# A third PSUM bank for every third accumulation of a product, borrowed from the attention

## The chip, the cores and the metric

The kernel runs on one core of a Trainium2 chip. The metric is the device time of one execution in microseconds (us). Time is told as the median of several runs; the profile is of one further execution.

## The reference

Three stages follow one another: an attention with a sliding window of 128 keys and four "sink" keys that every query sees, a dense layer with a maximum over three products (a maxout), and a mixture of eight experts in which tokens are assigned greedily by score, 384 to each expert.

```python
# q, k, v: 4 x 8 x 768 x 64
scores = scale * q @ k.T;  keep = is_sink | in_window
a = softmax(where(keep, scores, -1e9));  attn = a @ v
x = attn.transpose(0, 2, 1, 3).reshape(3072, 512)
h = maximum(maximum(x @ w1, x @ w2), x @ w3)      # 3072 x 768
x = h @ w_out                                     # 3072 x 512
logits = x @ w_gate                               # 3072 x 8
# greedy: by falling logit, a token takes the expert if it has room (384)
out[mask_e] = maximum(x[mask_e] @ u1[e], 0) @ u2[e]
```

All of it is in fp32. The kernel reaches that precision by splitting an operand into a high and a low part and adding three products (high by high, high by low, low by high).

## The kernel before, in words

The 3072 tokens are worked off in eight groups of 384 (`g` = 0 to 7). Each group needs four attention units ("pairs", two heads for half of a sequence). For a pair, `score` makes the scores (L138 to L141), which are copied with the mask into a tile T (L144 to L150); `soft` makes the softmax (L156 to L163); `pv` transposes the weights and multiplies them with the values (L166 to L201). In `pv` the weights of the sinks are transposed first, into the tile `pt` (L166, L167; the transposes run at L25): one PSUM bank, of which the pool `pst` has only one. ScalarE reads it at L169, then VectorE at L170, and with that the bank is free again.

The dense layer of a group has two parts. `group` makes the hidden rows: six slices of 128 columns, for each of them three products of 12 matmuls (L305) in the two banks of the tile `mm`, with the maximum taken on ScalarE and VectorE (L307, L308) and the split into high and low parts (L313, L314). `x2` multiplies the hidden rows with w_out: three blocks of 128 tokens, each in two halves of columns, so six accumulations of 18 matmuls (L330). Each accumulates in one bank of `mm` and is copied to the tile `xo` by ScalarE (L332), after which its bank may be written anew. In the middle groups (1, 0, 2, 3, 4 in this order of time) a half has 260 columns: 256 of the output and 4 of the logits, since w_out is kept with the product of w_out and w_gate beside it. Group 0's hidden rows were spilled to DRAM and come back one by one (L347 to L350) when group 1 is done. The last groups go other ways (L362, and L330 with 256 columns) and are not touched.

The eight PSUM banks are divided so in this part: `mm` 2, `pt` 1, `pp` 1 (transposed window weights), `ps` 3 (scores), `po` 1 (product with the values).

The order on each engine is not written out. It is made when the program is built: a scheduler lays instructions out over a simulated timeline, by their priority and as soon as their inputs and a free buffer are there. The four pairs of group g+1 are issued between the slices of group g (L698) with a higher priority, `off` = 60 (L681). On the chip every engine then works off its own queue in the order found, with semaphores for the waits.

Of the kernel before, what the change touches and what calls it, by code (L numbers as in the profile page):

```python
# [19 lines left out]
FT=mybir.dt.float32; FR=mybir.dt.float32r; BF=mybir.dt.bfloat16; I32=mybir.dt.int32; U8=mybir.dt.uint8; U32=mybir.dt.uint32  # L20
AF=mybir.ActivationFunctionType; OP=mybir.AluOpType; AX=mybir.AxisListType
NEG=-8.0e9
def f32(ap): return ap.bitcast(FT)
# [11 lines left out]
class Attn:  # L35
    def __init__(s, tc, q,k,v,vs, keep, consts, pst, psp, pss, psv, work):
        s.tc=tc; s.nc=nc=tc.nc; s.q,s.k,s.v,s.vs=q,k,v,vs
        s.pst,s.psp,s.pss,s.psv,s.w=pst,psp,pss,psv,work
        jp=work.tile([128,128],I32,name="jp",tag="qs0",bufs=2)
        nc.gpsimd.iota(jp,pattern=[[1,128]],base=0,channel_multiplier=-1)  # L40
        s.ident=keep.tile([128,128],FR,name="ident")
        nc.vector.tensor_scalar(s.ident,jp,0.0,None,op0=OP.is_equal)
        s.ca=consts.tile([128,2,128],U8,name="ca")
        nc.vector.tensor_scalar(s.ca[:,0,:],jp,0.0,None,op0=OP.is_le)
        nc.vector.tensor_scalar(s.ca[:,1,:],jp,0.0,None,op0=OP.is_gt)
        s.ul=consts.tile([128,2,128],BF,name="ul")
        nc.vector.tensor_scalar(s.ul[:,0,:],jp,0.0,None,op0=OP.is_lt)
        nc.vector.tensor_scalar(s.ul[:,1,:],jp,0.0,None,op0=OP.is_ge)
        s.negs=consts.tile([128,2,4],FT,name="negs"); nc.vector.memset(s.negs,NEG)

        s.vk=[]; s.pb=[]
        for i in range(2):
            t=consts.tile([128,2,128],FR,name=f"vk{i}"); nc.vector.memset(f32(t),0.0); s.vk.append(t)
            t=consts.tile([128,384],FR,name=f"psb{i}"); nc.vector.memset(f32(t),0.0); s.pb.append(t)
        s.kf=[]; s.ql=[[consts.tile([128,384],FR,name=f"ql{h}") for h in range(2)]]
        t=consts.tile([1,1],FT,name="one"); nc.vector.memset(t,0.0)
        nc.scalar.activation(t,t,AF.Exp)
        s.behind=None; s.ev={}; s.n=0; s.no=('kh0','kh1')
        s.extra=None
# [159 lines left out]

class Moe1:  # L220
    def __init__(s, tc, words,wgate, consts, wpool, main, conv, mm, pt, pss, ident):
        s.tc=tc; s.nc=tc.nc; s.mm=mm; s.pss=pss; s.main=main; s.conv=conv; s.ident=ident; s.consts=consts
        s.src=words; s.wgate=wgate
        s.W=[[wpool.tile([128,4,768],FR,name=f"w{i}{x}") for x in "hl"] for i in range(3)]
        s.WO=None; s.at=None; s.stage=None; s.HL=None; s.nx=0; s.second=None; s.n=0; s.loads=[]
        s.WG=main.tile([128,6,16],FR,name="wgt")
# [92 lines left out]
    def x2(s,H,t0,LG,x2d,n=260,pool=None,keep=None):  # L319

        nc=s.nc; main=s.main; mms=[]
        for t in range(3):
            o=pool.tile([128,512],FT,name="xq",bufs=4) if pool else s.room(t).tile([128,520],FT,name="xo",bufs=1)
            for u in range(2):
                c=slice(0,260) if n==260 else slice(4-4*u,260-4*u)
                ps=s.mm.tile([128,512],FT,name="mm")
                k=0
                for f in range(6):
                    for a,b in ((0,0),(0,1),(1,0)):
                        mms.append(nc.tensor.matmul(ps[:,:n],H[f][a][:,t*128:(t+1)*128],s.WO[b][:,f,u,c],start=(k==0),stop=(k==17))); k+=1  # L330
                with s.tc.high_priority():
                    nc.scalar.activation(o[:,u*n:(u+1)*n],ps[:,0:n],AF.Copy)  # L332
                    if keep is not None:
                        for d in (2*u,2*u+1):
                            h,l=keep(t,d); c=ps[:,(d-2*u)*128:(d-2*u)*128+128]
                            nc.scalar.activation(h,c,AF.Copy)
                            nc.vector.tensor_tensor(l,c,f32(h),op=OP.subtract)
            if n==260:
                o,e=s.row(o,0)
                nc.scalar.activation(LG[:,t0+t,:].rearrange("p (u e) -> p u e",u=2),e,AF.Copy)  # L340
            nc.scalar.dma_start(x2d[(t0+t)*128:(t0+t+1)*128,:],o)
        return mms
# [474 lines left out]
```

## Time and profile before

| what | value |
| --- | --- |
| median of 3 runs | 962.07 us (961.85 to 962.66) |
| the profiled execution | 963.42 us |
| its span, first to last instruction | 961.6 us |
| TensorE busy (PE) | 927.3 us, 96% of the span |
| VectorE busy (DVE) | 705.2 us, 73% |
| ScalarE busy (ACT) | 487.7 us, 51% |
| GpSimd busy (POOL) | 257.1 us, 27% |
| mean granted TensorE clock | 0.992 |

Times in the rows count from the start of the span. A row of a timeline has the start, the duration, the engine, the line of the kernel, the operation, the tile written and the tile read, and the count; in brackets stands how long the engine was idle just before and what ended that. Names such as `T_w` and `T_x` are two buffers of the same tile, and `HL` holds the hidden rows. The five calls of `x2` with 260 columns lie at 173.8 to 193.5 us (group 1), 195.8 to 224.1 (group 0), 279.6 to 296.4 (group 2), 347.8 to 366.3 (group 3) and 417.8 to 434.8 (group 4).

### The profile page before, as it was taken

To read this page: it belongs to the slowest core of one execution; us is meant where nothing else is said; L and a number is where in the kernel's file an instruction comes from. 1 tells how busy PE (TensorE), PEld (TensorE's weight loads), DVE (VectorE), ACT (ScalarE), POOL (GpSimd) and SP (SyncE) were. 2 spreads that over 40 slices of the span, in tenths; PEclk is the share of its full clock that TensorE was granted. 3 is DMA by queue.
4 is the path that set the end of the run, shared out by engine and by line. 5 is a ranking of instruction groups with operands and counts; after the bars stand their busy time and mean duration, and the time that the engine had idled before them with its cause. 6 is when DMAs were issued, how large, how long until landed. Compare 5 with 4: busy or idle time off the path is not lost.

```text
span 961.6 us, 18493 instructions
## 1 busy us (share of the span) xinstructions
PE 927.3 (96%) x6552; PEld 850.4 (88%) x6552; DVE 705.2 (73%) x1867; ACT 487.7 (51%) x1329; POOL 257.1 (27%) x271
## 2 busy tenths in 40 slices
PE   5999899989999999999999999999999999999996
PEld 4688799979999999999999998888888888888895
DVE  7776787687887886778896445888989889874320
ACT  5366474687677675676674211334434434344431
POOL 4676536132321312211231000011103022054321
PEclk9999899999999999999999999999999999999999
DMA  7454321242123121122210002544345353454410
GB/s 233 137 191 144 105 93 64 81 145 68 52 63 94 41 85 57 44 79 85 81 57 1 1 1 88 192 145 132 111 154 176 103 169 119 151 194 156 142 66 33
DMA packets 54443, 99.35 MB, mean 103 GB/s; under 512 B 7792, under 2 KB 24688, under 8 KB 54352
## 3 DMA queue, kind: packets, MB, share of 16 engines
q1 hardware_dynamic: 44464, 75.90, 25.3%
q0 software_dynamic: 3840, 12.45, 3.7%
q10 hardware_dynamic: 6048, 9.83, 2.7%
q8 instruction: 51, 0.84, 0.4%
q14 instruction: 40, 0.33, 0.1%
HBM read 82.17 MB, written 16.12 MB: 102 GB/s over the span
## 4 chain that ended last, share of the span: by engine, by line
PE 82%; DVE 6%; issue 5%; ACT 3%; DMA 2%; POOL 1%; SPq 0%; POOLq 0%; ACTq 0%; DVEq 0%
PE mm L305 28%; PE mm L634 13%; PE acc L627 12%; PE mm L330 8%; PE po L198 3%; PE rc L432 3%; PE po L188 2%; PE pt L25 2%; PE ps L138 2%; PE pp L25 2%; PE ps L140 1%; PE ps L141 1%; PE acc L362 1%; PE po L199 1%; DMA qf<-in_q_dram 1%
## 5 line engine op out<-in xcount | busy, mean ns | idle before, releaser
L627 PE MATMUL acc<-wbh,HL 128*128 128x512 f32 x384 | 133.1, 401 | 0.1
L308 DVE TENSOR_TENSOR hm<-mm,hm 128x384 f32<-128x384 f32 x96 | 53.2, 554 | 50.7 <-PE mm L305 49.5
L330 PE MATMUL mm<-woh,HL 128*128 128x260 f32 (+1 forms) x432 | 86.0, 289 | 2.7 <-ACT xo L332 1.2
L627 PEld LDWEIGHTS acc<-wbh,HL 128*128 128x128 f32 x384 | 71.4, 188 | 12.6 <-ACT HL L637 0.4
L578 ACT ACTIVATE wah<-sa 128x512 fp32r<-128x512 f32 x64 | 40.5, 632 | 82.2 <-PE mm L634 69.3
L578 ACT ACTIVATE wbh<-sb 128x512 fp32r<-128x512 f32 x64 | 40.4, 631 | 72.8 <-PE acc L627 68.9
L627 PE MATMUL acc<-wbl,HL 128*128 128x512 f32 x192 | 76.5, 398 | 0.0
L646 POOL DMA_INDIRECT out_dram<-og,idx x24 | 29.3, 1221 | 168.7 <-ACT og L645 165.9
L330 PEld LDWEIGHTS mm<-woh,HL 128*128 128x128 f32 x432 | 68.4, 188 | 4.7 <-ACT xo L332 1.9
L634 PE MATMUL mm<-HL,wah 128*128 128x384 f32 x256 | 67.5, 341 | 0.0
L305 PE MATMUL mm<-xh,w2h 128*128 128x384 f32 x192 | 66.8, 348 | 0.2 <-ACT hm L307 0.2
L305 PE MATMUL mm<-xh,w1h 128*128 128x384 f32 x192 | 66.1, 344 | 0.8 <-ACT hm L307 0.5
L305 PE MATMUL mm<-xh,w0h 128*128 128x384 f32 x192 | 66.5, 346 | 0.0
L305 PE MATMUL mm<-xl,w0h 128*128 128x384 f32 x192 | 65.4, 341 | 0.0
L305 PE MATMUL mm<-xl,w2h 128*128 128x384 f32 x192 | 65.4, 340 | 0.0
L305 PE MATMUL mm<-xh,w2l 128*128 128x384 f32 x192 | 65.3, 340 | 0.0
L305 PE MATMUL mm<-xh,w1l 128*128 128x384 f32 x192 | 65.3, 340 | 0.0
L579 DVE TENSOR_TENSOR wbl<-sb,wbh 128x512 fp32r<-128x512 f32 x64 | 45.2, 706 | 27.1 <-ACT wbh L578 27.0
L305 PE MATMUL mm<-xh,w0l 128*128 128x384 f32 x192 | 64.9, 338 | 0.0
L305 PE MATMUL mm<-xl,w1h 128*128 128x384 f32 x192 | 64.8, 338 | 0.0
L638 DVE SCALAR_TENSOR_TENSOR HL<-mm,HL 128x384 fp32r<-128x384 f32 x64 | 35.5, 554 | 38.1 <-ACT HL L637 37.8
L163 POOL TENSOR_TENSOR T_w<-T_w,l 128x792 f32<-128x792 f32 x21 | 32.7, 1559 | 108.0 <-DVE l L162 108.0
(334 smaller groups left out, 2815.8 us busy)
## 6 DMA issues: line engine op xcount, KB each, us to landing
sa<-in_u_dram SPq DMA_DIRECT2D x64, 256.0 KB
sb<-in_u_dram SPq DMA_DIRECT2D x64, 256.0 KB
HL<-in_words_dram SPq DMA_DIRECT2D x18, 512.0 KB
qn<-in_q_dram SPq DMA_DIRECT2D x88, 96.0 KB
x2d<-xo ACTq DMA_DIRECT2D x15, 256.0 KB
kn<-in_k_dram SPq DMA_DIRECT2D x12, 264.0 KB
st<-in_words_dram SPq DMA_DIRECT2D x6, 512.0 KB
vn<-in_v_dram SPq DMA_DIRECT2D x12, 256.0 KB
```

The lines of the kernel that those rows point to most:

```text
L25: nc.tensor.transpose(out,x,f32(ident))
L163: s.ev['s',u['n']]=nc.gpsimd.tensor_tensor(T,T,l[:,:,None].to_broadcast([128,6,132]),op=OP.mult)
L198: nc.tensor.matmul(po[:,q:q+n],u['VS'][:,blk,128*h:128*h+128],part[:,c:c+n],start=(part is H and j==0),stop=False,skip_group_check=True)
L305: nc.tensor.matmul(ps[:,:384],s.W[i][a][:,p,f*128:(f+1)*128],X[p][b],start=(n==0),stop=(n==11)); n+=1
L308: else: nc.vector.tensor_tensor(m,ps[:,:384],m,op=OP.max)
L330: mms.append(nc.tensor.matmul(ps[:,:n],H[f][a][:,t*128:(t+1)*128],s.WO[b][:,f,u,c],start=(k==0),stop=(k==17))); k+=1
L578: nc.scalar.activation(h,src,AF.Copy)
L579: (nc.gpsimd if s.n>=6 and nm=="wa" else nc.vector).tensor_tensor(l,src,f32(h),op=OP.subtract)
L627: s.mms.append(nc.tensor.matmul(acc[t],H[f][a][:,t*128:(t+1)*128],W[f][1][b],start=(f==0 and n==0),stop=(f==F-1 and n==2))); n+=1
L634: s.mms.append(nc.tensor.matmul(ps[:,:384],W[f][0][a][:,k,:],X[k][b],start=(n==0),stop=(n==11))); n+=1
L638: nc.vector.scalar_tensor_tensor(l,ps[:,:384],0.0,f32(h),op0=OP.max,op1=OP.subtract)
L646: st=nc.gpsimd.indirect_dma_start(out=s.out,out_offset=bass.IndirectOffsetOnAxis(ap=idx[:,t:t+1],axis=0),in_=o,in_offset=None)
```

## The change

In `x2`, with 260 columns, the third and the sixth accumulation of a group take the tile `pt` from the pool `pst` in place of a tile `mm`. The pool of that name is given to `Moe1` already and only has to be kept. The operations, their shapes, their operands and their number stay the same.

```diff
 class Moe1:
     def __init__(s, tc, words,wgate, consts, wpool, main, conv, mm, pt, pss, ident):
-        s.tc=tc; s.nc=tc.nc; s.mm=mm; s.pss=pss; s.main=main; s.conv=conv; s.ident=ident; s.consts=consts
+        s.tc=tc; s.nc=tc.nc; s.mm=mm; s.pss=pss; s.pt=pt; s.main=main; s.conv=conv; s.ident=ident; s.consts=consts
...
             for u in range(2):
                 c=slice(0,260) if n==260 else slice(4-4*u,260-4*u)
-                ps=s.mm.tile([128,512],FT,name="mm")
+                ps=s.pt.tile([128,512],FT,name="pt") if n==260 and (2*t+u)%3==2 else s.mm.tile([128,512],FT,name="mm")
                 k=0
```

## Rows read from the trace of the kernel before

**Rows 1.** The page's first part: busy time of the engines, share, instructions.

```profile
PE 927.3 (96%) x6552; PEld 850.4 (88%) x6552; DVE 705.2 (73%) x1867; ACT 487.7 (51%) x1329; POOL 257.1 (27%) x271
```

**Rows 2.** Table of stretches; columns named in its first line.

```profile
core 0: us, PE busy (x) PEld busy (x) DVE busy (x) ACT busy (x) POOL busy (x), PEclk, DMA share, GB/s
...
200.00:224.50 24.50, 21.37 (x157) 18.90 (x156) 21.23 (x41) 19.98 (x73) 7.53 (x6) 1.00 0.40 124
224.50:279.60 55.10, 55.10 (x366) 54.79 (x366) 45.99 (x95) 38.93 (x118) 15.51 (x20) 1.00 0.21 60
347.80:366.50 18.70, 17.67 (x148) 17.39 (x146) 16.44 (x31) 14.06 (x46) 5.15 (x6) 1.00 0.31 97
417.70:434.60 16.90, 16.30 (x133) 15.83 (x133) 11.04 (x27) 12.85 (x46) 4.67 (x5) 1.00 0.26 84
434.60:512.00 77.40, 75.51 (x489) 73.48 (x488) 65.90 (x116) 53.05 (x163) 20.09 (x20) 1.00 0.22 67
```

**Rows 3.** TensorE's waits, 173 to 512 us: total, times, longest.

```profile
PE po L198 <- DVE x L201: 1.4, 2, 0.8
PE mm L330 <- ACT xo L332: 1.2, 2, 1.0
...
PE pp L25 <- DVE A_w L179: 0.5, 1, 0.5
```

**Rows 4.** Chain that ended last, near 220 us: start, duration, what (two accumulations).

```profile
219.66 4.39 PE mm L330 x36
```

**Rows 5.** Timelines of VectorE, ScalarE and TensorE in group 0's product.

```profile
203.59 0.55 DVE L170 TENSOR_TENSOR psb<-pt,psb 8x384 fp32r<-8x384 f32 x1
...
209.15 0.56 DVE L350 TENSOR_TENSOR HL<-hm,HL 128x384 fp32r<-128x384 f32 x1
...
213.66 0.55 DVE L29 TENSOR_TENSOR xl<-x,xh 128x384 fp32r<-128x384 f32 x1
...
211.25 0.66 ACT L332 ACTIVATE xo<-mm 128x260 f32<-128x260 f32 x2
...
210.79 0.39 PE L140 MATMUL ps<-kh_w,qs 128*128 128x260 f32 x1 [0.52 <-DVE T_w L150]
...
212.72 0.39 PE L140 MATMUL ps<-kh_w,qs 128*128 128x260 f32 x1 [1.43 <-DVE T_x L150]
```

**Rows 6.** Timelines of VectorE and TensorE ahead of and in group 4's product.

```profile
408.32 0.55 DVE L170 TENSOR_TENSOR psb<-pt,psb 8x384 fp32r<-8x384 f32 x1
...
423.05 0.50 PE L330 MATMUL mm<-woh,HL 128*128 128x260 f32 x2 [0.41 <-DVE HL L314]
...
424.14 0.39 PE L330 MATMUL mm<-woh,HL 128*128 128x260 f32 x1 [0.19 <-ACT xo L332]
```

**Rows 7.** Timelines of TensorE, VectorE and ScalarE in group 3's product.

```profile
351.62 0.49 PE L25 MATMUL pt<-ident,T_w 128*128 128x128 f32 x3
...
356.13 0.39 PE L330 MATMUL mm<-woh,HL 128*128 128x260 f32 x1 [1.03 <-ACT xo L332]
...
353.69 0.62 DVE L314 TENSOR_TENSOR HL<-hm,HL 128x384 fp32r<-128x384 f32 x1
...
356.29 0.55 DVE L170 TENSOR_TENSOR psb<-pt,psb 8x384 fp32r<-8x384 f32 x1
...
355.70 0.38 ACT L332 ACTIVATE xo<-mm 128x260 f32<-128x260 f32 x1
```

**Rows 8.** Timelines at the sixth accumulation of groups 1 and 4, and ahead.

```profile
191.21 0.28 PE L330 MATMUL mm<-woh,HL 128*128 128x260 f32 x1
...
192.55 0.55 DVE L170 TENSOR_TENSOR psb<-pt,psb 8x384 fp32r<-8x384 f32 x1
...
419.03 1.50 DVE L29 TENSOR_TENSOR xl<-x,xh 128x384 fp32r<-128x384 f32 x3 [0.63 <-ACT xh L28]
...
432.49 0.28 PE L330 MATMUL mm<-woh,HL 128*128 128x260 f32 x1
...
434.13 0.55 DVE L170 TENSOR_TENSOR psb<-pt,psb 8x384 fp32r<-8x384 f32 x1
```

## The prediction

> **What bounds the kernel now.** I read the busy shares first, then the table of stretches, then who waited for whom on TensorE, and last the timelines around the waits of the product with w_out. The reader is to see four things. First, TensorE is the bound: it is busy for 96% of the span [rows 1]. In the stretch from 224.5 to 279.6 us it never stops, while VectorE is at 46.0 of 55.1 us [rows 2]. So there is time to win only in stretches where PE's column is shorter than the stretch. Second, the stretches with the product `x2` in its 260-column form are among these. They are short by 24.50 - 21.37 = 3.13 us (group 0, whose hidden rows are reloaded), 18.70 - 17.67 = 1.03 us (group 3) and 16.90 - 16.30 = 0.60 us (group 4) [rows 2]. Groups 1 and 2 have nothing to give there. Third, waits of an `x2` matmul for its bank (released by the copy at L332) are only 1.2 us in all [rows 3]. The rest of what PE lacks in these stretches is input that is late. Fourth, the bank that the change borrows is held by the sinks' transposes for some microseconds each time, until L170 on VectorE has read it.
>
> **The change part by part.** Nothing is added or removed: no instruction, transfer or byte. Of the 30 accumulations of 18 matmuls (five groups, six each) ten write to the tile `pt` in place of `mm`: the third and the sixth of each group. An accumulation takes 4.39 / 2 = 2.20 us [rows 4]. What changes is who may hold which bank, and with it the order that the scheduler writes. That order is laid out by a simulated timeline, which the trace does not show; each site below therefore has two ends.
>
> Group 0, third accumulation. While the hidden rows come back one by one, only two accumulations can be open, in the two `mm` banks. When their last rows are ready (L350 at 209.15, for 0.56 us) and done, PE waits 0.52 us and 1.43 us for scores whose destination VectorE has not cleared, at 210.79 and 212.72 [rows 5]. The copies at L332 freed the `mm` banks from 211.25 on, for 0.66 us, that is by 211.91, and still no `x2` matmul ran before 212.72: it stood behind the waiting score matmul in the queue [rows 5]. With a third bank the third accumulation is open ahead of these waits. `pt` is free for it: L170 had read it by 203.59 + 0.55 = 204.14 [rows 5]. Its 2.20 us of matmuls fill 0.52 + 1.43 = 1.95 us. The ends are -3.13 (all of the stretch's idle time) and 0 (the scheduler still puts it behind the scores). I take -1.95, only the two waits that the timeline shows well after the release at 204.14. Does it last? The last split input of group 2 is done at 213.66 + 0.55 = 214.21 [rows 5], long before that group's first matmul at the end of the stretch, 224.5, so the matmuls of group 2 can follow earlier at once.
>
> Group 4, third accumulation. PE waits 0.41 us for the last hidden rows and 0.19 us for the copy that frees a bank [rows 6]. `pt` was last read at 408.32 [rows 6] and is free. A third open accumulation covers both: -0.60, with the other end at 0.
>
> Group 3, third accumulation. Here stands the longest bank wait, 1.03 us until 356.13, since the last hidden rows were split only by 353.69 + 0.62 = 354.31 and the copy at L332 came at 355.70 [rows 7]. This looks like the change's own case, but `pt` is taken: the sinks' transposes write it at 351.62, and L170, late in VectorE's queue, reads it from 356.29 to 356.84 [rows 7]. If the accumulation waits for that, it starts 356.84 - 356.13 = 0.71 us later than now. If it is put ahead of the transposes instead, the 1.03 us go and the attention pair waits for it. Ends -1.03 and +0.71. I take +0.35, half of the upper end, nearer to the late read, because the attention is traced with a higher priority (L681) and will mostly get the bank first.
>
> Sixth accumulations. In group 1 it starts at 191.21 and L170 lets `pt` go at 192.55 + 0.55 = 193.10. In group 4 it starts at 432.49 and the release is at 434.13 + 0.55 = 434.68 [rows 8]. So they would be 1.89 us and 2.19 us late if nothing else fills the time. I cost them at nothing: the cover is other ready TensorE work, in group 4 the next group's first product, whose inputs were split by 419.03 + 1.50 = 420.53 [rows 8]. If the cover is gone, because the matmuls already stand in the queue, they cost +1.89 and +2.19. At the sixth of the other three groups the trace shows no such overlap.
>
> What is queued behind: a matmul that waits for `pt` holds every later TensorE instruction, the scores and transposes of the attention among them. In the other direction, the sinks' transposes wait until L332 has copied an accumulation out; VectorE's L170 and the product with the sinks' values wait for them. A transposed bank that is 2.20 us late is covered while PE has other work, as it has from 224.5 to 279.6 [rows 2].
>
> The sum: -1.95 - 0.60 + 0.35 = -2.20 us. The profiled execution took 963.42 us, 1.8 us more than its span and 1.35 us above the median of the runs, 962.07. I set the difference on the median: 962.07 - 2.20 = 959.9 us. About 0.2%, 1.9 us, is what a measurement of this kernel can tell from no change; the forecast lies just beyond it.
>
> One rule of the skill points the other way. Of the waits, the row at 212.72 shows an `x2` accumulation with a free bank standing behind a waiting score matmul [rows 5]. The Trainium skill says the same of the engine (TensorE: Matmul & The Clock Gate, "The mechanism"): matmuls start and end strictly in program order. By that, a matmul that waits for the borrowed bank stops the whole engine; it is the second rival. The skill's page Perfetto Trace Analysis ("Matmuls") says that independent groups should rotate through different banks so that copying out overlaps; by that alone only the bank waits would go.
>
> **The rivals.** *Given back or not taken*: no change, 962.1. The accumulations get `pt` only after the transposes, so they sit where they are now; or the 1.95 us are won and lost again where VectorE ends last. For it: only 1.2 us are true bank waits, and in 434.6 to 512 us VectorE is busy 65.9 of 77.4 us [rows 2] and PE waits 1.4 us and 0.5 us for it there [rows 3]. Against it: between, PE runs without a gap.
>
> *TensorE stalls on the borrowed bank*: slower. One mechanism: the third of group 3 and the sixth of groups 1 and 4 stand in PE's queue before L170 has read the sinks' weights. Its price is 0.71 + 1.89 + 2.19 = 4.79 us with no fill, 966.9; with the fills of groups 0 and 4, 964.3. It decides when the order has no other ready matmul ahead of these accumulations, for L170 is late in VectorE's queue: in group 3 the bank is held from 351.62 to 356.84 [rows 7]. For it: three of the ten sites overlap a hold in the trace of before. Against it: the order is not fixed, and other work is ready at two of the three.
>
> *Everything fills*: 3.13 + 1.03 + 0.60 = 4.76 us, 957.3; this is the far end of the forecast's own case.
>
> **How the numbers follow.** The forecast's case (faster, 957.3 to 960.1) gets 0.42, no change 0.33, the stall 0.25 (around 965). The predicted time is that of the first, 959.9. Below 957.3 it could go only if the waits behind 434.6, 1.9 us [rows 3], fell away too: 955.4. The range leaves out about 1 in 10 on each side: 956.6 to 965.4. As cases of both signs hold weight, the forecast's own range, 957.3 to 960.1, stands beside it. Faster by over 0.2%: 0.42; within: 0.33; slower: 0.25.
>
> **What would show it.** Right: in the stretch of group 0 TensorE's idle time falls from 3.13 us to about 1.2, with `pt` written by L330 in the place of the waits at 210.79 and 212.72; the matmuls of L330 show no wait for ACT L332; the later stretches keep their length. Wrong: a wait of L330 for DVE L170 at groups 1, 3 or 4; a wait of L25's `pt` for L332 with VectorE idle after it; or new waits behind 434.6 us that take back what the first stretches gave. The prediction is wrong as a whole if the new order moves scores or softmax steps far from the sites that I listed, since I costed only these.

## The result, and the profile after

The changed kernel took 973.84 us (median of 5 runs, 972.11 to 974.66) against 962.44 us for the kernel before on the same chip: 1.0109 times as long, 95% interval 1.0091 to 1.0128. It is slower by 11.4 us, above the upper end of the range (965.4 us). The profiled execution took 972.38 us, with a span of 970.6 us, 9.0 us more than before.

The page's first part, kernel after; it answers to [rows 1].

```profile
PE 929.8 (96%) x6552; PEld 852.0 (88%) x6552; DVE 712.0 (73%) x1867; ACT 488.9 (50%) x1329; POOL 260.9 (27%) x271
```

The same 6552 matmuls, busy for 2.5 us more. The other 6.5 us of the 9.0 are idle time of TensorE: the span less PE's busy time was 961.6 - 927.3 = 34.3 us and is 970.6 - 929.8 = 40.8 us.

Where? I cut both traces at the same events: the first matmul of group 1's `x2`, the last matmul of group 0's `x2`, the first matmul of the experts (L634), the end. First the kernel before.

```profile
core 0: us, PE busy (x) PEld busy (x) DVE busy (x) ACT busy (x) POOL busy (x), PEclk, DMA share, GB/s
173.80:223.80 50.00, 46.87 (x344) 42.34 (x343) 39.52 (x86) 38.53 (x138) 11.48 (x10) 1.00 0.35 109
223.80:604.80 381.00, 376.12 (x2619) 367.94 (x2618) 277.41 (x596) 215.20 (x640) 70.84 (x86) 1.00 0.18 55
604.80:961.60 356.80, 346.96 (x2732) 304.10 (x2730) 258.40 (x899) 139.90 (x270) 77.26 (x64) 1.00 0.42 138
```

The same table, kernel after (columns as above).

```profile
173.40:232.70 59.30, 50.22 (x352) 43.68 (x352) 45.01 (x88) 41.56 (x149) 12.06 (x11) 1.00 0.32 97
232.70:614.30 381.60, 376.77 (x2610) 368.90 (x2609) 278.51 (x593) 213.34 (x628) 74.20 (x85) 1.00 0.18 54
614.30:970.60 356.30, 346.76 (x2732) 303.98 (x2730) 258.14 (x899) 139.95 (x270) 77.35 (x64) 0.99 0.43 138
```

The whole loss lies in the first stretch, "stage A" from here on: 59.30 - 50.00 = 9.3 us. The second, "stage B" (groups 2 to 7 and the routing), differs by 0.6 us, the third by 0.5 us. In stage A PE's idle time goes from 3.13 us to 59.30 - 50.22 = 9.08 us, 5.95 us more. A stretch between two events can take in more or less of the attention's work (here 352 matmuls, 344 before), so the idle time is the surer measure of the two. So the loss sits in the two groups that the prediction costed at 0 (group 1) and at -1.95 us (group 0).

What did TensorE wait for there? Its waits from 173 to 233 us, kernel after: waiting line and what ended the wait, then total us, times, longest. [rows 3] answers to it, for a longer stretch.

```profile
PE pp L25 <- DVE A_w L179: 4.1, 3, 2.6
PE mm L330 <- DVE HL L350: 2.1, 3, 1.3
PE mm L330 <- ACT HL L349: 1.6, 1, 1.6
PE ps L140 <- DVE T_w L150: 1.0, 2, 0.5
PE po L186 <- DVE psb L170: 0.2, 1, 0.2
```

Two things in the list were not in [rows 3] at that size: softmax weights (A_w) that are late, and the reloaded hidden rows (L349, L350). One thing is missing: no matmul of L330 waits for a bank, neither for L332 nor for the readers of `pt`, here or anywhere else in this trace. The timelines of TensorE, VectorE and ScalarE say why (kernel after).

```profile
187.85 0.49 PE L25 MATMUL pt<-ident,T_w 128*128 128x128 f32 x3
191.78 0.55 PE L25 MATMUL pp<-ident,T_w 128*128 128x128 f32 x3 [2.55 <-DVE A_w L179]
...
195.71 0.40 PE L140 MATMUL ps<-kh_x,qs 128*128 128x260 f32 x1 [0.42 <-DVE T_w L150]
...
196.06 0.49 PE L25 MATMUL pt<-ident,T_x 128*128 128x128 f32 x3
197.73 0.55 PE L25 MATMUL pp<-ident,T_x 128*128 128x128 f32 x3 [1.18 <-DVE A_w L179]
...
202.33 0.58 PE L186 MATMUL po<-psb,vk 128*128 128x384 f32 x2 [0.17 <-DVE psb L170]
...
204.07 0.39 PE L330 MATMUL pt<-woh,HL 128*128 128x260 f32 x1
...
208.49 0.29 PE L330 MATMUL pt<-woh,HL 128*128 128x260 f32 x1
...
192.16 0.55 DVE L170 TENSOR_TENSOR psb<-pt,psb 8x384 fp32r<-8x384 f32 x1
201.64 0.55 DVE L170 TENSOR_TENSOR psb<-pt,psb 8x384 fp32r<-8x384 f32 x1
...
208.94 0.94 ACT L349 ACTIVATE HL<-hm 128x384 fp32r<-128x384 f32 x2 [0.15 <-PE pt L330]
```

`pt` has four tenants here. Pair 10 writes it at 187.85 and L170 frees it at 192.16 + 0.55 = 192.71; pair 11 writes it at 196.06, free at 202.19. Only then comes the third accumulation of group 1, at 204.07, and then the sixth, at 208.49. From 192.71 to 196.06 the bank is empty, and TensorE is idle for 0.42 us of that time and for 1.18 us soon after it; but the third accumulation, whose hidden rows had long been ready (the fourth and fifth ran before it, in `mm`), doesn't take the bank. It comes after both pairs, as it does in the program: the loop at L696 writes pairs 10 and 11 ahead of group 1.

The later groups show the same from the other side. The program writes pairs 16, 20 and 24 (the first of groups 4, 5 and 6) behind the products of groups 2, 3 and 4. In the kernel before, where only pairs use `pt`, their sinks' transposes run at 269.42, 330.35 and 406.02 us, ahead of these products. In the kernel after they run at 304.00, 371.08 and 443.47 us, after the last matmul in `pt` of the product (300.00, 367.36 and 438.44 us). All tenants of `pt` in this part run in the order of the program there.

Behind group 1's late sixth hangs a second link. Group 0's reload writes the hidden rows `HL` that all six accumulations of group 1 read, so L349 at 208.94 waits for the sixth accumulation's tenant of `pt`. The reload's six splits, line by line: count, shortest/median/longest ns, first to last start. Kernel before:

```profile
L349 ACT ACTIVATE HL<-hm x6: 507/514/524, 193.6 to 207.6; 128x384 fp32r<-128x384 f32 x6
```

Kernel after:

```profile
L349 ACT ACTIVATE HL<-hm x6: 506/509/525, 208.9 to 221.7; 128x384 fp32r<-128x384 f32 x6
```

The reload starts 15.3 us later. In the time that it leaves, TensorE has only two pairs' attention, whose softmax it must wait for; afterwards it has too much of `x2` and waits for its input. The chain that ended last runs through just these (kernel after; start, duration, what).

```profile
202.92 1.23 PE po L188 x6
204.14 2.38 PE pt L330 x18
...
210.85 1.79 DVE HL L350 x2
...
223.09 2.23 DVE HL L350 x2
...
230.80 2.14 PE pt L330 x18
```

### The profile page after: what moved, and what is told of

Same layout as the page of the kernel before. It is cut to its first block, busy times and chain, and to the rows that moved or that the text cites. A ratio compares the mean times of both kernels' runs of the same rounds, so it can differ in the third digit from the quotient of the medians.

```text
span 970.6 us, 18494 instructions
## 1 busy us (share of the span) xinstructions
PE 929.8 (96%) x6552; PEld 852.0 (88%) x6552; DVE 712.0 (73%) x1867; ACT 488.9 (50%) x1329; POOL 260.9 (27%) x271
## 4 chain that ended last, share of the span: by engine, by line
PE 82%; DVE 6%; issue 5%; ACT 3%; DMA 2%; POOL 1%; POOLq 0%; ACTq 0%; DVEq 0%
PE mm L305 28%; PE mm L634 13%; PE acc L627 12%; PE mm L330 6%; PE po L198 3%; PE rc L432 3%; PE ps L138 2%; PE po L188 2%; PE pt L25 2%; PE pt L330 2%; PE pp L25 2%; DMA qf<-in_q_dram 1%; PE ps L140 1%; PE ps L141 1%; PE acc L362 1%
## 5 line engine op out<-in xcount | busy, mean ns | idle before, releaser
L634 PE MATMUL mm<-HL,wah 128*128 128x384 f32 x256 | 67.5, 341 | 0.0
L330 PE MATMUL mm<-woh,HL 128*128 128x260 f32 (+1 forms) x312 | 62.5, 290 | 4.1 <-DVE HL L350 2.1
L179 DVE TENSOR_TENSOR A_w<-pp,ul 128x768 f32<-128x768 f32 x54 | 51.2, 948 | 5.7 <-PE pp L25 4.3
```

What stands on the lines that cost most here:

```text
L179: nc.vector.tensor_tensor(A,pt[:,:384].rearrange("p (i q) -> p i q",q=128)[:,:,None,:].to_broadcast([128,3,2,128]), s.ul[:,None,:,:].to_br ...
L634: s.mms.append(nc.tensor.matmul(ps[:,:384],W[f][0][a][:,k,:],X[k][b],start=(n==0),stop=(n==11))); n+=1
```

## The experiments

The theory after this reading: **the bank goes to its tenants in the order in which the program first writes them**, whoever is ready; so group 1's accumulations wait for pairs 10 and 11, and the reload for them. The rivals: TensorE stalls in its queue on the bank (the second rival of the prediction); the pairs get the bank by their higher priority; the loss comes from groups 0, 2, 3 or 4; or a third open accumulation costs by itself, whoever shares the bank. Each ratio is to the kernel before, timed on the same chip in the same series; its time differs between chips (962 to 972 us), so only ratios are compared. The edits change the condition in L326, where `t0` is 3 in group 1, 0 in group 0, and 6, 9, 12 in groups 2 to 4.

| what takes `pt` | median us (before) | ratio | 95% interval |
| --- | --- | --- | --- |
| the change: all five groups, third and sixth | 973.84 (962.44) | 1.0109 | 1.0091 to 1.0128 |
| g1_only: group 1 | 987.46 (971.10) | 1.0185 | 1.0161 to 1.0208 |
| not_g1: groups 0, 2, 3, 4 | 970.32 (971.10) | 0.9991 | 0.9974 to 1.0007 |
| g1_third: the third of group 1 | 988.27 (971.10) | 1.0198 | 1.0170 to 1.0227 |
| g1_sixth: the sixth of group 1 | 987.01 (971.10) | 1.0162 | 1.0131 to 1.0194 |
| claim_both: as the change, claimed earlier in group 1 | 976.05 (971.14) | 1.0036 | 0.9998 to 1.0074 |
| g1_g0: groups 1 and 0 | 985.96 (971.14) | 1.0159 | 1.0138 to 1.0181 |
| g0_only: group 0 | 975.44 (971.14) | 1.0044 | 1.0023 to 1.0065 |
| own_bank: a bank of its own, scores one less | 1000.39 (971.14) | 1.0291 | 1.0264 to 1.0318 |
| late_only: groups 2, 3, 4 | 963.14 (962.52) | 1.0014 | 0.9997 to 1.0030 |
| not_g0: groups 1 to 4 | 979.92 (962.52) | 1.0182 | 1.0166 to 1.0198 |
| pss2: none, scores one bank less | 979.54 (962.52) | 1.0172 | 1.0153 to 1.0191 |
| g0_third: the third of group 0 | 961.28 (963.77) | 0.9974 | 0.9959 to 0.9989 |
| claim_not_g0: claim_both without group 0 | 966.54 (963.77) | 1.0036 | 1.0016 to 1.0056 |
| thirds: the thirds of groups 0, 2, 3, 4 | 966.60 (972.35) | 0.9935 | 0.9910 to 0.9960 |

### Which group loses: g1_only and not_g1

```diff
-                ps=s.pt.tile([128,512],FT,name="pt") if n==260 and (2*t+u)%3==2 else s.mm.tile([128,512],FT,name="mm")
+                ps=s.pt.tile([128,512],FT,name="pt") if n==260 and t0==3 and (2*t+u)%3==2 else s.mm.tile([128,512],FT,name="mm")
```

> Only group 1's third and sixth accumulation take the bank pt. Theory A (the third accumulation of group 1 stands behind the sinks' transposes of two pairs, and the reload of group 0's hidden rows cannot begin before it): the whole loss is here, about +8 to +10 us, and the first row of the reload (L349) starts near 209 us as in the changed kernel, 15 us later than before. Theory B (the new order costs a little in every group): +2 to +4 us. Theory C (it is group 0's own product with three open accumulations): within 1 us of before.

```diff
+                ps=s.pt.tile([128,512],FT,name="pt") if n==260 and t0!=3 and (2*t+u)%3==2 else s.mm.tile([128,512],FT,name="mm")
```

> Groups 0, 2, 3 and 4 take the bank pt, group 1 stays in mm. Theory A: the loss is gone, within 3 us of before (my first forecast's fill in group 0 then gives up to -2 us). Theory B: +5 to +8 us. Theory C: the full +9 to +11 us.

Measured: group 1 alone costs 1.85%, more than the whole change; without it nothing is lost (0.9991, interval across 1). Stage A of g1_only (table of stretches, columns as above):

```profile
172.40:240.30 67.90, 57.57 (x395) 50.46 (x394) 55.21 (x111) 51.36 (x182) 16.04 (x16) 0.97 0.33 97
```

Stage A of not_g1:

```profile
173.00:219.00 46.00, 44.63 (x328) 40.38 (x327) 34.13 (x76) 34.85 (x127) 11.22 (x10) 1.00 0.37 111
```

With group 1 in the bank the reload starts at 207.9 us; without it, at 192.8. TensorE's idle time in stage A is 67.90 - 57.57 = 10.33 us with it and 46.00 - 44.63 = 1.37 us without it, 3.13 us before. (The lengths, 17.9 us more and 4.0 us less than before, overstate this: 395 and 328 matmuls fall into the stage, 344 before.) So the place is group 1, as theory A had it, and group 0 gains 1.8 us in stage A.

The size was not as expected: +8 to +10 us was written down, and the ratio gives 18 us, more than the whole change. In stages A and B together, up to the experts, g1_only takes 447.3 us where the kernel before takes 431.0, for the same 2963 matmuls. Of these 16.3 us TensorE is idle for 8.7 and busy for 7.6: the matmuls themselves are slower. The granted clock of stage A is 0.97 there, and 1.00 in the kernel before and in the change. So part of this loss is TensorE's clock, which the last section comes back to.

### The third or the sixth: g1_third and g1_sixth

```diff
+                ps=s.pt.tile([128,512],FT,name="pt") if n==260 and t0==3 and 2*t+u==2 else s.mm.tile([128,512],FT,name="mm")
```

> Only the third accumulation of group 1 takes the bank pt. Theory A: this one is enough, +6 to +10 us, since all six accumulations must have read the hidden rows before the reload. Theory B: under +2 us.

```diff
+                ps=s.pt.tile([128,512],FT,name="pt") if n==260 and t0==3 and 2*t+u==5 else s.mm.tile([128,512],FT,name="mm")
```

> Only the sixth accumulation of group 1 takes the bank pt. Theory A: if it stands behind the same transposes, as late as the third did, +5 to +10 us; if it waits only for one reading by L170, as I had put it, +1.9 us at most. Theory B: under +2 us.

Either one alone costs about what both cost: 1.0198 and 1.0162 beside 1.0185. In g1_third the third accumulation runs at 205.79, after pair 11's transposes at 197.91; in g1_sixth the sixth runs at 206.16, after pair 11's at 200.92. The reload starts at 206.3 and 207.3 us, and stage A takes 67.8 and 66.6 us. Costs of two stalls would add up; a delay until one event, the release by pair 11, does not. One late accumulation is enough, since the reload needs all six. Here too the sizes were missed: at most +10 us was expected of each, and the ratios give 19 and 16 us. The granted clock of stage A is 0.95 and 0.92.

### The same bank, claimed earlier: claim_both

If the order of first writes is the cause, a first write that stands earlier must move the accumulation, with nothing else changed. Here four columns of the tile are set to zero ahead of pair 10 (for the third) and ahead of pair 11 (for the sixth); the accumulations use these tiles. The two writes cost 62 ns each on VectorE.

```diff
-                    for o in order1.split(): emit(o,True)
+                    for o in order1.split():
+                        if o=='a2':
+                            for j in {1:(2,),2:(5,)}.get(cnt['a2'],()):
+                                M.early[j]=pst.tile([128,512],FT,name="pt"); nc.vector.memset(M.early[j][:,0:4],0.0)
+                        emit(o,True)
...
-                ps=s.pt.tile([128,512],FT,name="pt") if n==260 and (2*t+u)%3==2 else s.mm.tile([128,512],FT,name="mm")
+                ps=s.early[2*t+u] if t0==3 and 2*t+u in s.early else s.pt.tile([128,512],FT,name="pt") if n==260 and (2*t+u)%3==2 else s.mm.tile([128,512],FT,name="mm")
```

> The change, and on VectorE a memset of 4 columns of the bank pt for group 1's third accumulation ahead of pair 10's code and one for its sixth ahead of pair 11's; the accumulations then write these tiles. Theory A (the bank goes to its tenants in the order of their first write in the program, whoever is ready, so that pairs 10 and 11 come before group 1's third): the tenants now come as pair 9, third, 10, sixth, 11; L349 starts near 194 us again and the loss goes, between -3 and +3 us of before. Theory B' (holding the bank so long is what costs, in either order): +6 us or more.

Measured: 1.0036 in place of 1.0109; some two thirds of the loss are gone, by the middle of an interval that is wide (0.9998 to 1.0074). That is 3.5 us, just outside the 3 us expected. Its stage A (columns as above) and its timelines (TensorE, ScalarE):

```profile
172.20:221.40 49.20, 45.86 (x326) 41.07 (x326) 40.10 (x84) 36.92 (x135) 10.81 (x10) 0.97 0.38 112
...
180.97 0.28 PE L330 MATMUL pt<-woh,HL 128*128 128x260 f32 x1
...
187.62 0.49 PE L25 MATMUL pt<-ident,T_w 128*128 128x128 f32 x3
...
195.38 0.28 PE L330 MATMUL pt<-woh,HL 128*128 128x260 f32 x1
...
196.84 0.94 ACT L349 ACTIVATE HL<-hm 128x384 fp32r<-128x384 f32 x2
```

The row at 180.97 is the last matmul of group 1's third accumulation, now ahead of pair 10's transposes; the row at 195.38 belongs to the sixth, between the two pairs. The reload starts at 196.84, 12.1 us earlier than in the change, and group 0's `x2` ends at 221.4 us (223.8 before, 232.7 in the change). TensorE's idle time in stage A is 49.20 - 45.86 = 3.34 us: 9.08 in the change, 3.13 before. This is the run that shows the mechanism: same bank, same matmuls, and the pairs keep their higher priority, so it is not priority that gave them the bank. What moved is the place where the program takes the tile and first writes it. The two moved together, so which of them sets the order isn't told apart; and the two short writes on VectorE are new. What remains, 0.36%, lies mostly behind stage A: TensorE's idle time in stage B is 7.35 us there, 4.88 before.

### How the groups add up: g1_g0, g0_only, not_g0, late_only

```diff
+                ps=s.pt.tile([128,512],FT,name="pt") if n==260 and t0<=3 and (2*t+u)%3==2 else s.mm.tile([128,512],FT,name="mm")
```

> Groups 1 and 0 take the bank pt, groups 2 to 4 don't. Group 1 alone cost 18 us and the whole change 10.5 us, so something gives 7 us back. If it is the third open accumulation while group 0's rows come late: about +10.5 us. If it is the later groups: about +18 us.

```diff
+                ps=s.pt.tile([128,512],FT,name="pt") if n==260 and t0==0 and (2*t+u)%3==2 else s.mm.tile([128,512],FT,name="mm")
```

> Only group 0's third and sixth accumulation take the bank pt. My forecast's fill of 1.95 us alone: -2 us. Theory A adds that the sinks' transposes of pair 12, which stood ahead of group 0's third in the trace of before (213.07 us), must now wait for its sixth, some 10 us: 0 to +2 us.

```diff
+                ps=s.pt.tile([128,512],FT,name="pt") if n==260 and t0!=0 and (2*t+u)%3==2 else s.mm.tile([128,512],FT,name="mm")
```

> Groups 1 to 4 take the bank pt, group 0 stays in mm. If the parts add up: 18.0 - 5 = +13 us; the whole change, with group 0, was +10.5 us.

```diff
+                ps=s.pt.tile([128,512],FT,name="pt") if n==260 and t0>=6 and (2*t+u)%3==2 else s.mm.tile([128,512],FT,name="mm")
```

> Only groups 2, 3 and 4 take the bank pt. Without group 1 the whole was -0.9 us, group 0 alone +4.3 us, so these three should give -5 us if the parts add up; if the parts only reorder by chance, between -2 and +3 us.

Measured, with the tables of stretches cut at the same events:

| run | ratio | stage A us (matmuls) | idle in A | clock in A | stage B us | idle in B |
| --- | --- | --- | --- | --- | --- | --- |
| before | 1 | 50.0 (344) | 3.13 | 1.00 | 381.0 | 4.88 |
| the change | 1.0109 | 59.3 (352) | 9.08 | 1.00 | 381.6 | 4.83 |
| g1_only | 1.0185 | 67.9 (395) | 10.33 | 0.97 | 379.4 | 6.37 |
| g1_g0 | 1.0159 | 60.6 (351) | 8.09 | 0.94 | 385.8 | 9.57 |
| not_g0 | 1.0182 | 67.9 (395) | 9.10 | 0.95 | 379.5 | 8.43 |
| g0_only | 1.0044 | 45.9 (328) | 1.30 | 1.00 | 389.5 | 8.49 |
| late_only | 1.0014 | 50.0 (344) | 3.14 | 1.00 | 380.6 | 4.91 |

(g1_only and not_g0 ran on different chips and have the same stage A, so the stages can be compared across chips.) The parts don't add up, and most of these expectations were missed. Groups 1 and 0 together cost 15.4 us, where about 10.5 or about 18 was expected; groups 1 to 4 cost 17.5 us, where 13 was; group 0 alone costs 4.3 us, where 2 was the most. Groups 2 to 4 alone change nothing that can be told (interval across 1), where -5 us would have been the sum. From group 1 alone to the whole change some 7 us are given back, but group 0 gives back little without groups 2 to 4 (1.0185 to 1.0159), and they give back nothing without group 0 (1.0182). Both together do; these runs don't say why. What shows it is stage B, where the change idles for 4.83 us and g1_g0 for 9.57.

In stage A group 0's banks take 2.2 us of idle time away when group 1 is late (g1_only and g1_g0) and 1.8 us when it isn't (before and g0_only). But group 0 alone ends 0.44% slower. Its second stretch (g0_only, columns as above):

```profile
220.00:609.50 389.50, 381.01 (x2634) 372.36 (x2633) 284.14 (x605) 219.77 (x650) 72.93 (x87) 0.99 0.18 55
```

And a row of its TensorE timeline:

```profile
223.69 0.49 PE L25 MATMUL pt<-ident,T_w 128*128 128x128 f32 x3
```

Stage B is 389.5 us, 8.5 us more than the 381.0 of before. Of these 3.6 us are idle time, and 15 matmuls more fall into it. The row at 223.69 are the sinks' transposes of pair 12. In the kernel before they stand at 213.07, in the midst of group 0's product; here they come after group 0's sixth accumulation, 10.6 us later (in the whole change only at 236.66). It is the same rule in the other direction: pair 12 is written in the program behind group 0's `x2`, so it waits for both of group 0's tenants. That this is what costs the time is not shown: the two long waits of TensorE in this stretch, 3.14 us until 428.60 and 2.45 us until 501.06, come some 200 us later, and the kernel before has neither.

### A bank that nobody shares: own_bank and pss2

All eight banks are in use, so a bank of its own can only come from the scores (three banks to two).

```diff
-        psp=A_("psp",1,space=PS); pss=A_("pss",3,space=PS); psv=A_("psv",1,space=PS)
+        psp=A_("psp",1,space=PS); pss=A_("pss",2,space=PS); psv=A_("psv",1,space=PS); own=A_("own",1,space=PS)
...
+        M.pt=own
```

> The change, but the third bank is one of its own, taken from the scores (ps 3 banks to 2), so that the sinks' transposes share nothing. Theory A: group 1's third is not late, L349 near 194 us; what the scores lose with two banks is unknown, 0 to +8 us. If sharing were not the cause, +10 us and more.

The control is the kernel before with two banks for the scores:

```diff
-        psp=A_("psp",1,space=PS); pss=A_("pss",3,space=PS); psv=A_("psv",1,space=PS)
+        psp=A_("psp",1,space=PS); pss=A_("pss",2,space=PS); psv=A_("psv",1,space=PS)
```

> The kernel before with two banks for the scores in place of three, and nothing else: the control for the run with a bank of its own (+28 us). If the scores' lost bank was the cause there, +20 to +30 us; if not, under +8 us.

Measured: 1.0291 against 1.0172 for the control. The lost bank of the scores is most of it, but the rest, some 1.2 points, goes against what I expected: a bank without other tenants should not have been worse than the control. In own_bank the reload starts early (197.5 us), so the loss found above is not there; where the 1.2 points come from these runs don't settle. They do show what kind of time it is: TensorE is busy for 945.6 us in own_bank and for 934.3 in pss2, for the same 6552 matmuls, at a mean granted clock of 0.975 and 0.986. So 11.3 of the 18.6 us between the two spans are slower matmuls; the two ran on different chips, and how much of it is the chip is open. The control missed its own forecast as well (+20 to +30 or under +8 us): it cost 16.6 us. The pair is inconclusive on what an unshared bank is worth. That a third open accumulation doesn't cost by itself is seen below instead, in group 0 (g0_third).

### The kernel before once more: before_again

```diff
+
+# again
```

> The kernel before, unchanged but for a comment, for its trace on this chip: the same order, and group 0's reload (L349) starting near 193 us.

A second trace of the kernel before, 960.82 us. Stage A takes 49.9 us, stage B 381.0, the rest 356.4: within 0.4 us of the first trace, so for one and the same order stage differences of microseconds between two traces can be read. A changed kernel also gets a new order in the later groups, and what that does to stage B can't be told from the effect of the edit by one trace.

### Group 0 without its sixth: g0_third

```diff
+                ps=s.pt.tile([128,512],FT,name="pt") if n==260 and t0==0 and 2*t+u==2 else s.mm.tile([128,512],FT,name="mm")
```

> Only group 0's third accumulation takes the bank pt; its sixth stays in mm. If the sinks' transposes behind the sixth were what took the fill back (group 0 with both was +4.3 us), this is -2 to +1 us: the stretch to the end of group 0's product 4 us shorter, and what follows as before. If any gain there is lost later whatever the order, +3 to +5 us again.

Measured: 0.9974 (0.9959 to 0.9989), 2.5 us faster. Its first two stretches:

```profile
173.80:221.90 48.10, 46.45 (x343) 42.22 (x343) 36.95 (x82) 37.96 (x136) 11.35 (x10) 1.00 0.35 107
221.90:603.10 381.20, 375.64 (x2619) 367.39 (x2618) 278.02 (x600) 215.94 (x642) 73.61 (x86) 1.00 0.19 56
```

Stage A is 1.9 us shorter and stage B stays at 381.2 us. Pair 12's transposes come at 218.04. So the third of group 0 earns about what the prediction said (1.9 us, not the 4 us expected here), and with the sixth the gain is lost later: 0.9974 without it, 1.0044 with it. By which way the sixth costs it is not shown.

### The claim without group 0: claim_not_g0

```diff
+                ps=s.early[2*t+u] if t0==3 and 2*t+u in s.early else s.pt.tile([128,512],FT,name="pt") if n==260 and t0!=0 and (2*t+u)%3==2 else s.mm.tile([128,512],FT,name="mm")
```

with the rest as in claim_both.

> As claim_both, but group 0 stays in mm. If group 0's third bank caused what was left of the loss there (+3.5 us), -3 to +1 us. If the held bank or group 1 caused it, +3 us or more.

Measured: 1.0036, as claim_both. By the expectation this points to group 1 or the held bank, and not to group 0's third. Here group 0's `x2` ends at 227.1 us, 3.3 later than before, and stage B takes 380.8 us, as before. Stage A is 54.1 us, 4.1 more than before, for 340 matmuls in place of 344. Only 1.2 us of that are idle time (4.35 us); the rest is TensorE busy for longer, at a granted clock of 0.94. It fell after waits of 1.67 us (until 191.87) and 1.50 us (until 212.96): the slices of 4 us from 192 and from 212 us have 0.68 and 0.74. So the claim brings the idle time of stage A near to its old size, and what is left of the loss in this trace is mostly the clock. In the trace of claim_both it is idle time in stage B.

### The version that the runs point to: thirds

No group 1, no sixths: the third of groups 0, 2, 3 and 4.

```diff
+                ps=s.pt.tile([128,512],FT,name="pt") if n==260 and t0!=3 and 2*t+u==2 else s.mm.tile([128,512],FT,name="mm")
```

> Groups 0, 2, 3 and 4, the third accumulation alone. With the sixth as well this was -0.9 us, group 0's third alone was -2.5 us. If the sixth is what takes the gain back everywhere: -3 to -6 us. If the later groups have nothing to give: -1 to -3 us.

Measured: 0.9935 (0.9910 to 0.9960), faster than the kernel before by 5.8 us (966.60 against 972.35), in the range expected if the sixths take the gain back, and faster than the change by more. Its first two stretches:

```profile
174.20:221.90 47.70, 46.43 (x344) 42.19 (x343) 36.93 (x82) 37.94 (x136) 11.32 (x10) 1.00 0.35 108
221.90:598.70 376.80, 374.85 (x2619) 367.35 (x2618) 283.02 (x600) 216.64 (x642) 74.52 (x86) 1.00 0.19 56
```

PE's idle time is 1.27 us in stage A (3.13 before) and 1.95 us in stage B (381.00 - 376.12 = 4.88 before): together 4.8 us less. The waits of TensorE in stage B (thirds; total, times, longest):

```profile
PE mm L305 <- ACT hm L307: 0.8, 2, 0.5
...
PE mm L330 <- ACT xo L332: 0.2, 1, 0.2
```

The bank wait of [rows 3], 1.2 us, is 0.2 us, and the waits of L198 for L201, 1.4 us there, are not in the list. The first is what the third bank is for. The second lay at 479.58 and 505.65 us, behind group 4's product, so it may have gone by the new order alone. That the sixths are what keeps groups 2 to 4 from gaining is read from two sums, not isolated: with third and sixth (late_only) stage B is 380.6 us, with the thirds (and group 0's, which alone left it at 381.2) 376.8, on another chip. That a lucky order of the later groups gave part of it is a rival that was not tested. Whether the third of group 1, claimed early, would add to it was not tried.

## Why the prediction was wrong, point by point

**What bounds the kernel: right, and not enough.** TensorE is the bound in both kernels (96%). "Groups 1 and 2 have nothing to give there" was true of a gain and was used as if it held for a loss. Stage A, with group 1's product, is 9.3 us longer in the change, and group 1's two banks alone cost 1.85% of the time.

**The step that failed: the list of sites.** I looked in the trace of before for places where an accumulation and a hold of `pt` overlap in time, and costed these. That is the wrong test: in these runs the order of the bank's tenants follows the program. Group 1's third accumulation was no site at all: in the trace of before the first five are over at 189.71 + 0.28 = 189.99, and pair 10's transposes run at 190.32. It could run so early only because it had a bank apart from theirs; in the program it stands behind pairs 10 and 11. Once it shares their bank, it runs at 204.07. The prediction's ground, that the attention "will mostly get the bank first" by its higher priority (L681), failed both ways. In group 1 the pairs come first because they are written first. In group 3, of which it was said, the accumulations come first, and pair 20 waits for them until 371.08. And the delay was sized by the lateness of one L170 (0.71 us in group 3).

**The sixth of group 1, costed at 0 with an upper end of +1.89 us.** The cover that the prediction counted on, other ready TensorE work, was not there: TensorE had two pairs whose softmax it waited for. Alone the sixth costs 987.01 - 971.10 = 15.9 us. The upper end was one hold of the bank (until 193.10); the true one is a hold of a second pair, and behind it the reload. That L349 overwrites what the accumulations of group 1 read stands in the part on the kernel before ("when group 1 is done"); the prediction asked who waits for a matmul in TensorE's queue, and not who waits for its operand to come free.

**The sixth of group 0: "no such overlap", so no cost.** The same error in the order. Pair 12's transposes stand at 213.07, ahead of the sixth in the trace of before and behind it in the program. They come at 223.69 in g0_only, and the difference between g0_only and g0_third is 0.7% of the time; what leads from the one to the other stays open.

**The third of group 0, -1.95 us: right, once it stands alone.** In g0_third stage A is 1.9 us shorter and the run 2.5 us (the interval is 1.1 to 4.0 us). In thirds the place of the two waits of [rows 5], 0.52 and 1.43 us, looks like this (TensorE's timeline):

```profile
208.64 0.28 PE L330 MATMUL pt<-wol,HL 128*128 128x260 f32 x1
...
213.04 0.39 PE L140 MATMUL ps<-kh_w,qs 128*128 128x260 f32 x1 [0.29 <-DVE T_x L150]
```

Matmuls of L330 into `pt` fill the time and 0.29 us of waiting is left. The prediction's mark for a right step was an idle time of about 1.2 us in group 0; stage A of g0_third has 48.10 - 46.45 = 1.65 us, that of thirds 1.27 us.

**The thirds of groups 3 and 4, +0.35 and -0.60 us: the first on the wrong end, the second right.** In the whole change no matmul of L330 waits for L332, which was the prediction's own mark of success, and the kernel is slower all the same. In thirds the wait of [rows 7], 1.03 us, is down to 0.20 us:

```profile
353.23 0.39 PE L330 MATMUL mm<-woh,HL 128*128 128x260 f32 x1 [0.20 <-ACT xo L332]
```

The third accumulation of group 3 holds `pt` there ahead of pair 20, whose transposes come at 357.64. That is the lower end of the prediction's two (-1.03), which it passed over for the reason above. Group 4's waits of [rows 6], 0.41 and 0.19 us, are gone in thirds, as forecast.

**The rivals.** *Given back or not taken* had the order of group 1 right ("only after the transposes") and the consequence wrong: the accumulations did not stay where they were. The stall on the borrowed bank (966.9 us at most) had the sign right, and with the sixth of group 1 one of the sites; its price was wrong. Its own mark, a wait of L330 for L170, appears nowhere in the trace of the kernel after. The matmuls already stand behind the bank's release in TensorE's queue, so the time shows up as waits of the attention for its softmax (4.1 us) and of the late product for its input (3.7 us). A price for a wait in the queue was the wrong kind of price. The last sentence of the prediction named the true case, an order moved far from the listed sites, and gave it neither a time nor a share of the range. That is why the range ended 8.4 us too low.

## What to carry to other kernels

Before two producers share a buffer, list its tenants in the order of the program's first writes, and compare that with their order in the trace: whatever runs ahead of its place in the program (as group 1's third did ahead of pairs 10 and 11) will be held back to it. Then ask what hangs on the last reader of the held work's operands; a delay of one accumulation in six held up a whole reload. What is held back costs nothing where TensorE has other work: in thirds pairs 12, 16, 20 and 24 are late as well (pair 20 at 357.64 us, 330.35 before), and that kernel is the fastest. There the extra bank is worth what the waits beside it say: 1.9 us of stage A for one accumulation in group 0. With four it is 0.65%, of which stage B's share is not isolated.

## What the runs showed of the hardware that was not expected

**The clock after a wait.** In the kernel after, TensorE waits once for 3.15 us in group 5, and its timeline then reads:

```profile
489.32 0.34 PE L305 MATMUL mm<-xh,w2l 128*128 128x384 f32 x1
489.50 0.34 PE L305 MATMUL mm<-xh,w2h 128*128 128x384 f32 x1
...
497.55 0.43 PE L305 MATMUL mm<-xh,w0h 128*128 128x384 f32 x1 [3.15 <-DVE hm L308]
...
498.10 0.52 PE L305 MATMUL mm<-xh,w0l 128*128 128x384 f32 x1
498.42 0.52 PE L305 MATMUL mm<-xh,w0h 128*128 128x384 f32 x1
```

The table of stretches for the 4 us behind it (columns as above):

```profile
498.00:502.00 4.00, 4.00 (x19) 3.77 (x19) 3.64 (x9) 2.24 (x6) 0.00 (x0) 0.60 0.45 161
```

Ahead of the wait the matmuls start every 0.18 us, after it every 0.32 us; the granted clock from 498 to 502 us is 0.60, near the lower of its two levels, 1.2 of 2.4 GHz. Cut into slices of 4 us, the kernel before has none below 0.97 between 112 and 956 us. So this wait cost more than itself.

The length of a wait did not decide it in these runs. In not_g0 TensorE waits at the same place as in the kernel after (the row at 191.78 above), and just as long:

```profile
191.41 0.55 PE L25 MATMUL pp<-ident,T_w 128*128 128x128 f32 x3 [2.55 <-DVE A_w L179]
...
192.00:196.00 4.00, 4.00 (x15) 2.47 (x14) 3.80 (x7) 1.97 (x10) 2.52 (x3) 0.61 0.14 53
```

Its granted clock from 192 to 196 us is 0.61; in the kernel after it is 1.00 there. The same waits can thus cost one run more than another, and the runs with group 1 late (stage A at 0.92 to 0.97) lost time in this way that the change itself (1.00) did not.

**Chips.** The stretch from the first matmul of the experts to the end, the same 2732 matmuls in every kernel, takes 356.3 us in not_g0 and 364.7 us in g1_only, on another chip; the difference between the chips' times for the kernel before (962 and 971 us) is of about that size. The kernel before was not profiled on the slower chip. TensorE's and VectorE's instructions have the same order there in all traces. In g1_only 7.2 of the 8.4 us are waits of TensorE for a step of the routing on VectorE (L432 for L427), which not_g0 doesn't have at all; the other traces from chips where the kernel before takes 971 us or more have 6.4 to 8.6 us of it. L427 itself takes as long on both (559 and 558 ns), so what delays it stays open.
